# Four weight sums placed elsewhere in the DVE order, and the last sum of h moved between two output sums

## The chip, the cores and the metric

The kernel runs on one core of a Trainium2 chip. The metric is the device time of one execution in microseconds (us). The core has five engines that work through their own instruction streams and wait for each other by semaphores: PE (TensorE, matmuls), DVE (VectorE), ACT (ScalarE), POOL (GpSimd) and SP (SyncE, which issues most transfers).

## What is computed

Retention (attention with a decay instead of a softmax) over 8 batches, 8 heads, 576 positions, 64 features a head. Its output, 4608 tokens of 512 features, goes through four experts, each a two-layer network of width 1024, and the results are summed with weights for each token.

```
scores = (q @ k.T) / sqrt(64)
ret    = scores * where(i >= j, gamma[h] ** (i - j), 0)
x      = (ret @ v), heads side by side            # [4608, 512]
p      = domain_probs / (sum over experts + 1e-9)
for e in range(4):
    h    = maximum(x @ w1[e], 0)                  # [4608, 1024]
    out += p[:, e] * (h @ w2[e])                  # [4608, 512]
```

Inputs and output are float32; the matmuls work on bfloat16.

## The kernel before

**Tiles and stages.** Tokens are cut into 9 blocks of 512 (`nt` 0 to 8). A stage (nt, e) is one block and one expert. Its first layer (x to h, transposed as `hT`) is computed in stage (nt, e); its second layer (h to the output) is computed while PE works on the first layer of the following stage, so that the two alternate on PE.

**Two ways to multiply.** The first stages, up to the first layer of (1,0), are "classical": `up_classical` (L490) and `down_groups` (L538). They consist of 56 groups, numbered 0 to 55, and a list `plan` says which other work is put behind which group. From (1,1) on the first layer is done with a Strassen-like scheme of seven products instead of eight (`up_fast`, L652), the second layer likewise (`Down`, L594), expert by expert as their sums become ready (`begin`, L971). Such products need sums of operands, which DVE makes:
- `weight_sums` (L550) for w1, into `wsum`;
- `down_sums` (L572) for w2, into `dsum`: three sums (L562 to L564), and one difference written back into w2 (L565), each of 128 x 1024 elements;
- `token_sums` (L567) for x, into `tsum`, through the same lines L562 to L565 but with 128 x 512 elements;
- `hidden_sum` (L577) for h: sum 1 (L586), sum 2 (L588), an in-place difference (L590) and sum 4 (L592). Sums 1 and 2 are made in two halves, one for each group of a stage. The second half of sum 1 reads what POOL has just clipped at zero (L686).

**A fast stage.** It has two groups, g = 0 and 1. In each, `up_fast` issues seven up products into the PSUM banks P, Q and R and calls `fill(1)` to `fill(4)` between them, which issue the seven down products of the stage before. The first DVE addition of a group (L677) reads bank P, and PE's third up product into P has to wait until it has. `fill(4)` ends the down products: products 3 and 4, and then `out(0)` and `out(1)` (L647, or L645 for expert 0; its `out(1)` is on ACT, L643), the two output sums that add the result in PSUM to `acc`. The next group's first down product writes the bank that `out(0)` reads. `sums(1)` to `sums(3)` place h sums, steps of the attention, and token sums for the next block (a list `front`) on DVE.

**Buffers that are shared in time.** `dsum` of expert e lies in buffer `w2s_e`. The raw k, q and v of chunk e of batch 1 lie there before (`raw_units(1)`). So the first down sum of expert 1 waits until POOL has cast chunk 1 of batch 1 (L279 for k and q, L281 for v). These casts are issued at group 25 (`begin1`); the loads behind them go through SP's queue.

**Order.** The order on each engine is that of the program: DVE works strictly through its own list. In the classical part `sums_at` puts sum i behind group g. Groups 24 to 31 are the first layer of (0,2), 32 to 35 its second layer (each evacuated by DVE, L524), 36 to 43 the first layer of (0,3), 44 to 47 its second layer, 48 to 55 the first layer of (1,0). The attention of batch 1 runs at groups 39 to 47: transposes `T(c)` at groups 39, 41, 43, 45, and scores, masks (L333), outputs and kv sums one group later. From stage (1,1) on the attention of batches 2 to 7 is a list of steps, `chain`, from which `window` takes the next one that is ready. When none is ready it takes a token sum from `front`.

Of the kernel before, what the change touches and what calls it, by code (L numbers as in the profile page):

```python
# [23 lines left out]
def kernel(  # L24
# [12 lines left out]
    N, E = moe_domain_probs.shape  # L37
# [474 lines left out]
    def downs(nt, e, ring):  # L512

        hT = hTs[nt, e]
        if e == 0:
            acc[nt] = [apool.tile([128, Dm], FP32, tag="acc", name="acc") for _ in range(NSUB)]

        def evacuate(po, ns, cols):
            t = nt * NSUB + ns
            pe, a = probs[:, e, t:t + 1], acc[nt][ns][:, cols]  # L520
            if e == 0:
                nc.scalar.activation(a, po, Copy, scale=pe)
            else:
                nc.vector.scalar_tensor_tensor(a, po, pe, a, op0=MULT, op1=ADD)  # L524
            if e == E - 1:
                eng = nc.scalar if cols.start else nc.sync
                eng.dma_start(out=out[t * 128:(t + 1) * 128, cols], in_=a)

        for ns in range(NSUB):
            w = Dm // 2 if (nt, ns, e) == (n_nt - 1, NSUB - 1, E - 1) else Dm  # L530
            for d in range(0, Dm, w):
                po = bank(ring, [128, w], FP32, "po")
                for fc in range(NFC):
                    nc.tensor.matmul(po, lhsT=hT[:, fc, ns * 128:(ns + 1) * 128],  # L534
                                     rhs=w2_sb[e][:, fc, d:d + w], start=(fc == 0), stop=(fc == NFC - 1))
                    yield None if fc < NFC - 1 else lambda: evacuate(po, ns, slice(d, d + w))
# [30 lines left out]
    def token_sums(nt):  # L567
        x, a, b = xts[nt], slice(0, HT), slice(HT, NT)
        t = tsum[nt] = tpool.tile([128, 3, 2, HT], BF16, tag="ts", name="tsum", bufs=2)
        return right_sums(t, x[:, 0:2, a], x[:, 0:2, b], x[:, 2:4, a], x[:, 2:4, b])  # L570
# [6 lines left out]
    def hidden_sum(nt, e, i, g=None):  # L577

        lo, hi = (slice(2 * g, 2 * g + 2), slice(4 + 2 * g, 6 + 2 * g)) if g is not None else (slice(0, 4), slice(4, 8))
        hT = hTs[nt, e]  # L580
        a11, a12, a21, a22 = (hT[:, k, t] for t in (slice(0, HT), slice(HT, NT)) for k in (lo, hi))
        h = hsum.setdefault((nt, e), {})
        if i != 3 and i not in h:
            h[i] = hpool.tile([128, NFC // 2, HT], BF16, tag=f"hs{i}", name="hsum", bufs=1)
        if i == 1:
            nc.vector.tensor_tensor(h[1][:, lo], a21, a22, op=ADD)  # L586
        elif i == 2:
            nc.vector.tensor_tensor(h[2][:, lo], h[1][:, lo], a11, op=SUB)  # L588
        elif i == 3:
            nc.vector.tensor_tensor(a21, a11, a21, op=SUB)  # L590
        else:
            nc.vector.tensor_tensor(h[4][:, lo], a12, h[2][:, lo], op=SUB)  # L592

    class Down:  # L594
# [40 lines left out]
        def out(self, i, halves=(slice(0, 2),)):  # L635
# [3 lines left out]
            for x in halves:  # L639
# [8 lines left out]
                if self.e == E - 1:  # L648
                    eng = nc.scalar if len(halves) == 1 and x.start else nc.sync
                    eng.dma_start(out=out[t * 128:(t + 1) * 128, cols], in_=a)  # L650

    def up_fast(nt, e, g, fill, window, sums):  # L652

        x, T, w, s = xts[nt], tsum[nt], w1_sb[e], ssum[e]
# [17 lines left out]
        product(R_, lambda k: s[:, 0, k], lambda k: T[:, 0, k], start=True)  # L672
        nc.scalar.activation(m5, R_, Copy)  # L673
        fill(1)
        sums(1)
        product(P, lambda k: s[:, 1, k], lambda k: T[:, 1, k])
        nc.vector.tensor_tensor(R_, P, m5, op=ADD)  # L677
        product(Q, lambda k: w[:, 2 + k, :HF], lambda k: x[:, 2 + k, t0])
        nc.scalar.activation(hT[:, lo, t0], Q, Relu)  # L679
        fill(2)  # L680
        window("ACT")
        sums(2)
        product(P, lambda k: w[:, k, HF:], lambda k: x[:, k, t1])
        h22 = hT[:, hi, t1]
        nc.vector.tensor_tensor(h22, P, m5, op=ADD)  # L685
        nc.gpsimd.tensor_scalar(h22, h22, float("inf"), 0.0, op0=MIN, op1=MAX)  # L686
        product(R_, lambda k: s[:, 2, k], lambda k: x[:, 2 + k, t1])
        nc.scalar.activation(hT[:, lo, t1], R_, Relu)  # L688
        window("ACT")
        fill(3)  # L690
        sums(3)
# [183 lines left out]
    front = []  # L875

    def pool(nt, n):
        for _ in range(n):
            chain.emit("POOL", nt)
# [4 lines left out]
    def at(g, *fs):  # L884
        plan.setdefault(g, []).extend(fs)
# [52 lines left out]
    def sums_at(kind, e, *gs):  # L938
        todo = []
        for i, g in enumerate(gs):  # L940
            at(g, lambda i=i: (todo or todo.extend(kind(e)), todo[i]()))
        return todo
# [1 line left out]
    sums_at(weight_sums, 1, 16, 17, 18, 19)  # L944
    s0 = sums_at(weight_sums, 0, 20, 21, 22)
    sums_at(weight_sums, 2, 26, 28, 30, 31)
    sums_at(down_sums, 1, 32, 33, 34, 35)
    sums_at(weight_sums, 3, 36, 38, 49, 50)
    sums_at(down_sums, 2, 51, 52, 53, 54)
    at(50, lambda: a1().put_krem(nc.gpsimd, a1().qr[:, 1]))  # L950
# [5 lines left out]
    g = 0  # L956
# [14 lines left out]
    begin = {1: (1, 1), 2: (1, 2), 3: (2, 3), 0: (3, 0)}  # L971
# [6 lines left out]
    def pay(nt, e, late=False):  # L978
        for x in owed:
            if x[1] <= (nt, e) if late else x[0] <= (nt, e):  # L980
                owed.remove(x)
                x[2]()
                return True
        return False

    before, gaps = (1, 0), 0
    for nt, e in [(nt, e) for nt in range(1, n_nt) for e in range(E)][1:]:
        fast = before >= begin[before[1]]
        fill_classical = None if fast else downs(*before, "po")
        while pay(nt, e, late=True):  # L990
            pass

        def tokens(t):
            if t < n_nt and t not in tsum and chain.tokens >= (t + 1) * NT:
                front.extend(token_sums(t))

        def between(i):
            nonlocal gaps
            gaps += 1
            tokens(nt + 1)  # L1000
            if i == 3:
                pool(nt, 4 if gaps < 8 else 3 - g)
            if i == 3 or chain.todo["PE"] and "any" in chain.todo["PE"][0][1]:
                chain.emit("PE", nt)
            chain.now += 1

        def fill(i):
            if i == 4:
                chain.put_late()
            if not fast:  # L1010
                for _ in range(4):
                    f = next(fill_classical)
                    if f:
                        f()
            elif i == 1:
                state["d"] = Down(*before, g)
                d().product(1)
                d().product(5)
                d().copy("P1")
                d().copy("m5")  # L1020
            elif i == 2:
                d().product(6)
                d().copy("U")
                d().product(2, slice(0, 3))
            elif i == 3:
                d().product(2, slice(3, 4))
                d().product(7)
                d().add(12)
                d().add(22)
            else:  # L1030
                d().product(3)
                d().product(4)
                d().out(0)
                d().out(1)
            between(i)

        def d():
            return state["d"]

        def sums(i):  # L1040


            old, new = before in hsum, (nt, e) >= begin[e]
            turns = {(0, 1): 0 if old else 2, (0, 2): 0 if old else 1, (0, 3): 1,
                     (1, 1): 2, (1, 2): 1, (1, 3): 1}[g, i]
            if g == 0 and old:
                for a in {1: ((2, 1), (4,)), 2: ((3,),)}.get(i, ()):
                    hidden_sum(*before, *a)
            if g == 1 and new:
                for a in {2: ((1, 0), (2, 0)), 3: ((1, 1),)}.get(i, ()):  # L1050
                    hidden_sum(nt, e, *a)
            for _ in range(turns):
                window("DVE")
            chain.seen.update(chain.done)

        def window(kind):
            if chain.emit(kind, nt) or kind != "DVE":
                return
            if front:
                front.pop(0)()  # L1060
            else:
                pay(nt, e)

        while nt not in tsum:
            tokens(nt)
            if nt not in tsum:
                chain.put_late()
                moved = [chain.emit(k, nt, strict=False) for k in ("POOL", "PE", "DVE", "ACT")]
                assert any(moved), (nt, chain.done, {k: v[:1] for k, v in chain.todo.items()})
        chain.put_late()  # L1070
        while front and e == 0:
            front.pop(0)()
        for g in range(2):
            up_fast(nt, e, g, fill, window, sums)
        before = nt, e
# [49 lines left out]
```

## Time and profile before

| | us |
|---|---|
| median of 3 runs (527.42 to 527.99) | 527.7 |
| the profiled execution | 527.14 |
| its span, first to last instruction | 525.3 |

| engine | busy us | main work |
|---|---|---|
| DVE | 405.0 | additions and sums, masks, evacuations |
| ACT | 297.2 | evacuations with the nonlinearity |
| POOL | 180.8 | casts of k, q, v; clipping of h |

The span is the time between the first and the last instruction in the trace. The time of an execution is a little longer, since it includes what lies around it. Durations are read from this one execution.

Durations of what is touched: the down sums of 128 x 1024 take 0.68 to 1.41 us, the h sum L586 takes 0.41 to 1.25 us (median 0.42), an output sum of 128 x 512 takes about 0.74 us. The mean granted TensorE clock is 0.991 of full speed.

### The profile page before, as it was taken

What the parts mean: (1) busy time and instruction counts of PE and PEld (TensorE: products, weight loads), DVE (VectorE), ACT (ScalarE), POOL (GpSimd) and SP (SyncE); (2) the same over time, 40 slices, a digit from 0 to 9 for tenths busy, and PEclk for the clock granted to TensorE, in tenths of its full rate; (3) what the DMA queues carried; (4) which work ended last, traced back from release to release, by engine and by line L of the source; (5) the groups of instructions that cost most, each with busy time, mean ns of one, the idle gap of its engine ahead of it and who ended that gap; (6) DMA issues with size and microseconds to landing.
All of it is one profiled execution on the core that took longest, in us unless ns stands there. A gap on an engine that the chain in (4) does not pass through costs nothing.

```text
span 525.3 us, 12553 instructions
## 1 busy us (share of the span) xinstructions
PE 505.6 (96%) x4886; PEld 401.4 (76%) x4886; DVE 405.0 (77%) x744; ACT 297.2 (57%) x613; POOL 180.8 (34%) x275
## 2 busy tenths in 40 slices
PE   7999779999999999999999999999999999999995
PEld 3644335578767888888888888888888888888884
DVE  6614267969845889889888987899889987877786
ACT  3452143566546655666666656666666667666661
POOL 6702252634343343334433544353434310000010
PEclk9999979999999999999999999999999999999999
DMA  9999993954273253734384438523972020001002
GB/s 242 191 207 201 209 161 98 184 102 106 47 169 73 52 119 77 179 71 106 64 193 84 85 64 204 92 55 77 196 112 49 11 82 1 1 21 62 2 0 81
DMA packets 149836, 54.23 MB, mean 103 GB/s; under 512 B 131309, under 2 KB 144621, under 8 KB 149777
## 3 DMA queue, kind: packets, MB, share of 16 engines
q1 hardware_dynamic: 142448, 45.05, 40.5%
q0 software_dynamic: 7328, 8.39, 9.4%
q8 instruction: 38, 0.62, 0.5%
q14 instruction: 22, 0.17, 0.1%
HBM read 45.16 MB, written 9.44 MB: 104 GB/s over the span
## 4 chain that ended last, share of the span: by engine, by line
PE 77%; SPq 6%; DMA 5%; DVE 5%; issue 4%; POOL 2%; POOLq 0%; DVEq 0%
PE upP L665 19%; PE downV L616 18%; PE downW L616 12%; PE upR L665 9%; PE po L534 5%; PE upQ L665 5%; SPq L111 4%; PE ph L493 3%; DMA wt<-in_moe_w_dram 2%; DMA raw<-in_k_dram 2%; PE s L328 2%; SPq L105 1%; PE oc L372 1%; PE oc L369 1%; PE kvp L339 1%
## 5 line engine op out<-in xcount | busy, mean ns | idle before, releaser
L686 POOL TENSOR_SCALAR hT<-hT 128x512 bf16<-128x512 bf16 x62 | 38.2, 617 | 267.1 <-DVE hT L685 261.7
L665 PEld LDWEIGHTS <-wt 128*128 128x128 bf16 x992 | 94.9, 98 | 14.4 <-issue 0.5
L616 PEld LDWEIGHTS <-hT 128*128 128x128 bf16 x928 | 90.8, 98 | 12.9 <-issue 2.3
L665 PEld LDWEIGHTS <-wsum 128*128 128x128 bf16 x744 | 72.7, 98 | 11.8 <-issue 2.3
L616 PE MATMUL downV<-wt,hT 128*128 128x256 bf16 x464 | 78.4, 272 | 1.3 <-DVE acc L645 0.9
L665 PE MATMUL upP<-xT,wt 128*128 128x256 bf16 x496 | 74.4, 273 | 0.2
L616 PEld LDWEIGHTS <-hsum 128*128 128x128 bf16 x696 | 68.1, 98 | 8.4 <-issue 0.4
L693 ACT ACTIVATE hT<-upP 128x512 bf16<-128x512 f32 x62 | 37.0, 597 | 52.7 <-PE upP L665 41.1
L677 DVE TENSOR_TENSOR upR<-upP,m 128x512 f32<-128x512 f32 x62 | 43.2, 698 | 30.0 <-PE upP L665 17.3
L688 ACT ACTIVATE hT<-upR 128x512 bf16<-128x512 f32 x62 | 37.0, 597 | 41.4 <-PE upR L665 41.4
L534 PE MATMUL po<-wt,hT 128*128 128x512 bf16 x224 | 53.4, 379 | 0.0
L671 ACT ACTIVATE upQ<-upP 128x512 f32<-128x512 f32 x62 | 36.3, 586 | 26.2 <-PE upP L665 26.1
L685 DVE TENSOR_TENSOR hT<-upP,m 128x512 bf16<-128x512 f32 x62 | 42.7, 689 | 9.2 <-PE upP L665 8.5
L679 ACT ACTIVATE hT<-upQ 128x512 bf16<-128x512 f32 x62 | 37.0, 597 | 21.8 <-PE upQ L665 21.8
L509 ACT ACTIVATE hT<-ph 128x512 bf16<-128x512 f32 x40 | 23.5, 597 | 37.8 <-PE ph L493 37.8
L493 PE MATMUL ph<-xT,wt 128*128 128x512 bf16 (+3 forms) x180 | 38.1, 367 | 6.6 <-DVE acc L524 6.6
L647 DVE SCALAR_TENSOR_TENSOR acc<-downV,probs,acc 128x512 f32<-128x512 f32 (+1 forms) x48 | 34.4, 723 | 9.6 <-PE downV L616 9.4
L665 PE MATMUL upR<-tsum,wsum 128*128 128x256 bf16 x248 | 37.2, 273 | 1.9 <-DVE tsum L562 1.9
L333 DVE TENSOR_TENSOR sT<-s,tri 128x512 bf16<-128x512 f32 x56 | 36.8, 680 | 2.7 <-PE s L328 2.7
L586 DVE TENSOR_TENSOR hsum<-hT 128x512 bf16<-128x512 bf16 x58 | 35.5, 612 | 3.1 <-POOL hT L686 1.5
L673 ACT ACTIVATE m<-upR 128x512 f32<-128x512 f32 x62 | 36.8, 593 | 1.8 <-PE upR L665 1.8
L665 PE MATMUL upP<-tsum,wt 128*128 128x256 bf16 x248 | 37.3, 273 | 0.0
(134 smaller groups left out, 939.3 us busy)
## 6 DMA issues: line engine op xcount, KB each, us to landing
out_dram<-acc SPq DMA_DIRECT2D x32, 256.0 KB, 2.8
wt<-in_moe_w_dram POOLq DMA_DIRECT2D x6, 1024.0 KB, 25.2
raw_k<-in_k_dram SPq DMA_DIRECT2D x24, 256.0 KB, 3.4
raw_q<-in_q_dram SPq DMA_DIRECT2D x24, 256.0 KB, 3.6
raw_v<-in_v_dram SPq DMA_DIRECT2D x24, 256.0 KB, 3.7
raw<-in_k_dram SPq DMA_DIRECT2D x8, 256.0 KB, 5.0
raw<-in_q_dram SPq DMA_DIRECT2D x8, 256.0 KB, 5.5
raw<-in_v_dram SPq DMA_DIRECT2D x8, 256.0 KB, 5.5
```

The costliest lines, as they stand in the source:

```text
L333: nc.vector.tensor_tensor(self.sT[c][:, j], self.s[c][j], tri[:, :].unsqueeze(1).to_broadcast([128, NP, C]), op=MULT)
L493: nc.tensor.matmul(ph[:, ts], lhsT=w1_sb[e][:, dc, fc * 128:(fc + 1) * 128], rhs=xts[nt][:, dc, ts], start=(dc == 0), stop=(dc == NDC - 1))
L534: nc.tensor.matmul(po, lhsT=hT[:, fc, ns * 128:(ns + 1) * 128], rhs=w2_sb[e][:, fc, d:d + w], start=(fc == 0), stop=(fc == NFC - 1))
L616: nc.tensor.matmul(o, lhsT=l[:, k, self.s * 128:(self.s + 1) * 128], rhs=r[:, k], start=(i == 1 and k == 0), stop=(k == NFC // 2 - 1), ski ...
L665: nc.tensor.matmul(ps[:, l], lhsT=wa(kc)[:, f:f + 128], rhs=xa(kc), start=(start and l == 0 and kc == 0), stop=(kc == 1), skip_group_check ...
L673: nc.scalar.activation(m5, R_, Copy)
L677: nc.vector.tensor_tensor(R_, P, m5, op=ADD)
L679: nc.scalar.activation(hT[:, lo, t0], Q, Relu)
L685: nc.vector.tensor_tensor(h22, P, m5, op=ADD)
L686: nc.gpsimd.tensor_scalar(h22, h22, float("inf"), 0.0, op0=MIN, op1=MAX)
L688: nc.scalar.activation(hT[:, lo, t1], R_, Relu)
L693: nc.scalar.activation(hT[:, hi, t0], P, Relu)
```

## The change

Four sums on w2 of expert 1 get other places in the list of groups. The last half of h sum 1 is issued in `fill(4)` between `out(0)` and `out(1)` instead of in `sums(3)`; where the stage before was classical, it comes behind the fill. And in the second group of an expert 3 stage `window` takes a token sum first, if more than one is waiting, before a step of the attention.

```diff
-    sums_at(down_sums, 1, 32, 33, 34, 35)
+    sums_at(down_sums, 1, 42, 43, 44, 48)
...
                 d().product(4)
                 d().out(0)
+                last_sum()
                 d().out(1)
+            if i == 4 and not fast:
+                last_sum()
             between(i)
+
+        def last_sum():
+            if g == 1 and (nt, e) >= begin[e]:
+                hidden_sum(nt, e, 1, 1)
...
             if g == 1 and new:
-                for a in {2: ((1, 0), (2, 0)), 3: ((1, 1),)}.get(i, ()):
-                    hidden_sum(nt, e, *a)
+                for a in (1, 2) if i == 2 else ():
+                    hidden_sum(nt, e, a, 0)
...
         def window(kind):
+            if kind == "DVE" and len(front) > 1 and (e, g) == (E - 1, 1):
+                return front.pop(0)()
             if chain.emit(kind, nt) or kind != "DVE":
                 return
```

## The prediction

> **What bounds the kernel now.** I read the page first (busy shares, the clock row), then the waits, then the chain of waits in the stretch that stands out, then the timelines of the engines there and in the later, repeating stages.
>
> ```profile
> PE 505.6 (96%) x4886; PEld 401.4 (76%) x4886; DVE 405.0 (77%) x744; ACT 297.2 (57%) x613; POOL 180.8 (34%) x275
> PEclk9999979999999999999999999999999999999999
> ```
>
> The PE is the bound: only 19.7 of 525.3 us are without a matmul, so a change pays only where it fills one of those gaps or lifts the clock. One slice of 40 (65.7 to 78.8 us) has a lower clock. The waits name the largest single gap after the start:
>
> ```profile
> DVE dsum L562 <- POOL vm L281: 9.9, 1, 9.9
> PE ph L493 <- DVE acc L524: 6.6, 1, 6.6
> ```
>
> DVE stood 9.9 us before the first down sum, and PE 6.6 us for an evacuation queued behind it. The chain of waits from 54 to 80 us shows the order of causes:
>
> ```profile
> 54.23 9.95 DMA raw<-in_k_dram
> ...
> 66.55 0.62 POOL vm L281
> 67.17 0.02 issue
> 67.19 0.69 DVE dsum L562
> 67.88 0.67 DVE acc L524
> 68.55 0.04 issue
> 68.60 5.46 PE ph L493 x16
> ```
>
> A load of batch 1 lands late, POOL casts its chunk, the third cast frees the buffer that `dsum` of expert 1 takes over, and only then do the sum, the evacuation and the matmuls go. The table of windows gives the PE's loss and the clock:
>
> ```profile
> 62.00:68.60 6.60, 0.01 (x2) 0.00 (x1) 1.41 (x3) 0.00 (x0) 5.10 (x6) 0.76 1.06 213
> 68.60:74.00 5.40, 5.40 (x18) 2.02 (x18) 5.35 (x8) 1.79 (x3) 2.14 (x3) 0.66 1.26 202
> ```
>
> (columns: length, then busy us and count of PE, PEld, DVE, ACT, POOL, then clock, DMA share, GB/s). The stall has no PE work, and the matmuls after it run at 0.66 of the clock.
>
> The repeating stages have small gaps. Near the end of stage (3,1), that is nt 3, expert 1, which also finishes the products of (3,0), the timelines of POOL, DVE and PE have:
>
> ```profile
> 221.93 0.61 POOL L686 TENSOR_SCALAR hT<-hT 128x512 bf16<-128x512 bf16 x1 [4.50 <-DVE hT L685]
> 222.50 1.04 POOL L279 TENSOR_TENSOR km<-raw_k,gk 128x512 bf16<-128x512 f32 x1
> 223.50 1.22 POOL L279 TENSOR_TENSOR qm<-raw_q,gq 128x512 bf16<-128x512 f32 x1
> ...
> 222.57 1.25 DVE L586 TENSOR_TENSOR hsum<-hT 128x512 bf16<-128x512 bf16 x1
> 223.75 0.74 DVE L645 TENSOR_SCALAR acc<-downV,probs 128x512 f32<-128x512 f32 x1
> ...
> 224.54 0.60 PE L616 MATMUL downV<-wt,hT 128*128 128x256 bf16 x4 [0.21 <-DVE acc L645]
> ```
>
> L586 is the sum that moves. It took 1.25 us here, 0.42 in most places; the output sum behind it was late, and PE waited.
>
> **What the skill says, and the trace.** "TensorE: Matmul & The Clock Gate", Part 1, has the array fall to half clock after an idle window of about 3.4 us and return after about 3.4 us of sustained work. The trace agrees: the 6.6 us stall is followed by slow matmuls until about 72 us. "SBUF — State Buffer", Who interferes with whom, says that a DVE instruction with two SBUF inputs and a GpSimd instruction that reads SBUF exclude each other for a whole instruction. L586 has two such inputs; its 1.25 us ends 0.28 after the POOL cast that ran beside it, the time being the rest of the cast and its own 0.42 less overlap: the trace fits. "TensorE: Matmul & The Clock Gate", in its first table, calls VectorE's queue strict FIFO; the evacuation that waited behind L562 shows it.
>
> **Part 1: four down sums move from groups 32-35 to 42, 43, 44 and 48.** No instruction or DMA is added or dropped; in the listed order only DVE changes before 98 us.
> - Removed: the 6.59 us PE wait. Behind it 16 matmuls of 512 columns took 5.46; an earlier run of such matmuls (47.12 us) took 5.34 for 24, so 16 would be 3.56. That is 1.90 from the clock. Together 8.49 us.
> - What is late next: batch 1's transposes (group 39) would come at about 73.9 - 8.5 = 65.4. Casts are fed by loads and don't move: q of chunk 0 ends at 63.0, of chunk 1 at 66.5 (wanted at 68.3), of chunk 2 at 70.3 (wanted at 71.3). Chunk 3 was cast at 76.1 because km waited for kvp, not for its load; freed by an earlier kvp, it follows chunk 2 at about 71 to 75, wanted at 76.6. All have cover, of 1.0 us at the thinnest. Two casts landing later than I put them would give back what exceeds it.
> - The added wait: L562 in its new place comes at about 71, and its buffer is free at 67.2; no wait. Behind it are a transpose copy, masks and evacuations.
> - Where they land: each sum is 0.68 us alone, up to 1.41 beside POOL. DVE between 74 and 91 had gaps of 0.3 to 1.4 us and its consumers lie a group later (copy at 80.4, used at 82.1). I take 0; if cover fails, 0.7 each, 2.1 for three. The fourth enters a full DVE stretch (91.9 to 99.6) ahead of an idle 0.76: 0.68 to 1.26 less 0.76 is at most 0.5; I take 0.1.
>
> **Part 2: the last h sum goes between the two output sums (27 places, and behind the fill in two more).** The first output sum can start 0.64 us after its product's first matmul (499.66 to 500.30 near the end, DVE waiting).
> - Gain: at the end of stages (3,1) to (6,1) the first output sum moves up by 0.69 (223.75 to 223.06). PE's next product started 0.81 after the former instead of 0.44: 0.37 each, 1.5 us for four.
> - Cost: where the first output sum already waited for PE, the h sum filled an idle stretch and now does not. It delays L588, L592 and the next L677 by its pitch, 0.33 alone. L677 must start 0.74 before the third up product; from its idle time and that distance I get the spare: 0.34 in nt 7 and 8 (cost 0), 0.34 into (3,3) and (4,3) and 0.19 into (5,3) and (6,3), where POOL holds the sum longer (pitch 0.55: 0.1 each, 0.4), 0.15 into (3,1), (4,1) and (6,1) and 0.30 into (5,1) (a cast in the way, delay 0.40: 0.25 and 0.1, sum 0.85), 0.09 into the stages (6,0) and (7,0) (0.24 each, 0.5). Into (3,0) PE already waits 0.96 for `tsum`, queued behind: +0.35. Sum 2.1.
> - Net +0.6. Bounds: nothing but the gain, -1.5; or every contended sum at its longest (0.8 more in some 14 places less 0.3 spare, 7.0, less 1.5), +5.5. I take +0.6.
>
> **Part 3: token sums go first in the last group of expert 3.** At most two move up per block, and one attention step moves a slot later on PE in two blocks. No count changes. The stages after them lose one L564 from the crowded start, which pays for the h sum in (4,0) and (5,0), where PE waited 0.09 each. One mask goes before a later L677 that had 0.63 idle and 0.19 spare: covered. 0, bounds -0.5 and +0.7.
>
> **Sum.** -8.49 + 0.1 + 0.6 + 0 = -7.8. The profiled execution took 527.14 (span 525.3), so 519.3; the median of the runs shown, 527.7, is 0.56 above it: 519.9.
>
> **Rivals.**
> - Sums pay: contention moves away with the shift. Part 2 gives its 1.5 and part 3 0.5: 527.7 - 8.5 - 2.0 = 517.2 to 517.7. For it: POOL's casts are over in many places 0.7 us later. Against: spare is 0.15 or less in ten.
> - The casts become the bound: PE arrives 8.5 us earlier at transposes whose data come from the same loads. If a chunk is 3 us later than I put it, with the half clock risked again, 3 to 4 come back: 523.5. For it: load and cast ran back to back until 78 us. Against: the cast times above.
> - Slower: the moved h sum blocks. At the 19 places up to 412 us where POOL still casts, it would have to stand 1.25 each time, of which some 0.25 is spare: 19.0, less 1.5 and 8.5: +9.0, or 536.7. It decides from 0.53 a place beyond the spare ((8.5 + 1.5)/19). For it: it takes 1.25 in ten of them now. Against: in those it starts just behind a cast that POOL has begun, and 0.7 to 1.2 us later that cast is over.
> - The stall stays because something else frees the buffer: no change. The wait names only the cast, which ends before the new place.
>
> **How the numbers follow.** Forecast 0.68 (own range 518.2 to 521.8), sums pay 0.12, casts bind 0.14, slower 0.03, stall stays 0.03. The range reaches down into the first rival, where about half lies under it, and up to where some of the second is left out: 517.6 to 522.6. About 0.2% (1.1 us) can be told from no change here. Faster 0.94, same 0.03, slower 0.03.
>
> **What would show it.** Right: no wait of DVE L562 for POOL, no PE gap near 62 us, clock 1.00 through to the end, the first L665 near 89.5 instead of 97.9; no PE wait on L645; a longer wait before the first upR of stage (3,0). Wrong: PE waits on transposes or SPq between 65 and 90 us, or many short waits of upP for L677.

## The result and the profile after

| | before | after |
|---|---|---|
| median, us | 527.56 (4 runs, 527.41 to 527.99) | 521.48 (4 runs, 521.01 to 521.99) |
| the profiled execution, us | 527.14 | 521.01 |
| its span, us | 525.3 | 519.2 |

The ratio after to before is 0.9884, with a 95% interval from 0.9867 to 0.9901. The forecast was 519.9 with a range of 517.6 to 522.6: the side and the range held, and the median came 1.6 us above the forecast.

The page of the kernel after shows the busy time of the engines and the granted clock in 40 slices:

```profile
PE 503.8 (97%) x4871; PEld 400.7 (77%) x4886; DVE 401.6 (77%) x744; ACT 297.2 (57%) x613; POOL 180.6 (35%) x275
PEclk9999999999999999999999999999999999999998
```

The slice with the low clock near 70 us is gone (for the 8 at the end, the clock falls at 515.9 us, after the last matmul has ended at 513.8). The waits of PE in the kernel before (in total, times, longest, in us) had, beside the 6.6 us for L524:

```profile
PE upR L665 <- DVE tsum L562: 1.9, 2, 1.0
...
PE downV L616 <- DVE acc L645: 0.9, 4, 0.2
```

In the kernel after, the waits for L524 and for L645 are gone, that for `tsum` is longer, and those for L677 and L685 are new:

```profile
PE upR L665 <- DVE tsum L562: 2.3, 2, 1.3
...
PE upP L665 <- DVE upR L677: 0.9, 2, 0.7
PE downV L616 <- DVE acc L647: 0.4, 1, 0.4
PE upP L665 <- DVE hT L685: 0.4, 2, 0.2
```

The windows over the old stall, in the kernel after (length, busy us and count of PE, PEld, DVE, ACT and POOL, clock, DMA share, GB/s):

```profile
62.00:68.60 6.60, 6.55 (x51) 3.30 (x51) 4.19 (x6) 4.21 (x8) 4.74 (x5) 1.00 1.00 203
68.60:74.00 5.40, 5.35 (x61) 2.99 (x62) 4.33 (x8) 3.52 (x7) 4.41 (x5) 1.00 0.98 210
```

PE is busy for nearly all of both stretches (6.55 of 6.60 and 5.35 of 5.40 us), at full clock. To see where each 0.1 us went, I measured the distances between the same PE instructions in each kernel's trace. They start at the first `orem` matmul (the attention's output for the last 64 positions of the first batch, about 60 us), since what lies before it differs by up to 1.5 us between executions whatever the kernel. A group is marked by its first upR matmul. The column of the kernel before has the lengths, the others what each kernel takes more or less, in us:

| stretch on PE | before | after | p1_only | p1_p2 | p1_p3 | choose |
|---|---|---|---|---|---|---|
| `orem` to the transposes of group 39 (the stall) | 14.13 | -8.60 | -8.60 | -8.60 | -8.60 | -8.60 |
| on to the first upR of (1,1) | 24.48 | 0.00 | +0.02 | 0.00 | 0.00 | 0.00 |
| on to the second group of (1,1) | 7.58 | +0.61 | +0.77 | +0.61 | +1.02 | +0.43 |
| on to the second group of (2,3) | 83.47 | -0.19 | +0.01 | -0.18 | +0.02 | +0.02 |
| on to the first upR of (3,0) | 8.37 | +0.33 | 0.00 | +0.33 | 0.00 | 0.00 |
| on to the second group of (8,3) | 309.29 | +1.42 | 0.00 | +1.20 | +1.59 | -1.20 |
| from `orem` to the end of the span | 465.51 | -6.44 | -7.80 | -6.68 | -5.98 | -9.35 |

So the change gained 8.60 at the stall and lost 2.2 elsewhere. The other four columns are experiments. In the stretch to the second group of (1,1), the kernel after, p1_only, p1_p2 and p1_p3 still issue the same instructions: 0.61 to 1.02 there is what one program shows in four executions.

### The profile page after: what moved, and what is told of

Its sections match the earlier page's. It is cut to its first block, busy times and chain, and to the rows that moved or that the text cites. A ratio compares the mean times of both kernels' runs of the same rounds, so it can differ in the third digit from the quotient of the medians.

```text
span 519.2 us, 12541 instructions
## 1 busy us (share of the span) xinstructions
PE 503.8 (97%) x4871; PEld 400.7 (77%) x4886; DVE 401.6 (77%) x744; ACT 297.2 (57%) x613; POOL 180.6 (35%) x275
## 4 chain that ended last, share of the span: by engine, by line
PE 88%; DVE 7%; issue 2%; DMA 1%; ACT 1%; SPq 0%; DVEq 0%
PE upP L665 20%; PE downV L616 18%; PE downW L616 13%; PE upR L665 10%; PE po L534 9%; PE ph L493 7%; PE upQ L665 4%; PE s L328 2%; DVE upR L677 2%; DVE acc L647 2%; PE oc L372 1%; PE oc L369 1%; PE kvp L339 1%; DMA raw<-in_q_dram 1%; DVE hsum L586 1%
## 5 line engine op out<-in xcount | busy, mean ns | idle before, releaser
L677 DVE TENSOR_TENSOR upR<-upP,m 128x512 f32<-128x512 f32 x62 | 43.2, 696 | 25.0 <-PE upP L665 14.4
L534 PE MATMUL po<-wt,hT 128*128 128x512 bf16 x214 | 52.1, 379 | 0.6
L647 DVE SCALAR_TENSOR_TENSOR acc<-downV,probs,acc 128x512 f32<-128x512 f32 (+1 forms) x48 | 34.6, 726 | 21.6 <-PE downV L616 21.5
L685 DVE TENSOR_TENSOR hT<-upP,m 128x512 bf16<-128x512 f32 x62 | 42.7, 689 | 6.7 <-PE upP L665 4.7
L665 PE MATMUL upP<-tsum,wsum 128*128 128x256 bf16 x248 | 37.2, 273 | 0.0
L665 PE MATMUL upQ<-xT,wt 128*128 128x256 bf16 x248 | 37.2, 273 | 0.0
```

Of the source, the lines that this page charges most:

```text
L647: nc.vector.scalar_tensor_tensor(a, src, pe, a, op0=MULT, op1=ADD)
L665: nc.tensor.matmul(ps[:, l], lhsT=wa(kc)[:, f:f + 128], rhs=xa(kc), start=(start and l == 0 and kc == 0), stop=(kc == 1), skip_group_check ...
```

## The experiments

**Which part gives, which takes.** Theory A: Part 1 alone gives the whole gain, and parts 2 and 3 together lose. Theory B: Part 1 gives less, since POOL's casts bind behind the stall, and parts 2 and 3 gain. Two kernels: Part 1 alone, and parts 2 and 3 without it.

```diff
# p1_only: the kernel before, with
-    sums_at(down_sums, 1, 32, 33, 34, 35)
+    sums_at(down_sums, 1, 42, 43, 44, 48)
# p23_only: the kernel after, with
-    sums_at(down_sums, 1, 42, 43, 44, 48)
+    sums_at(down_sums, 1, 32, 33, 34, 35)
```

> Only the four down sums move; the last h sum and the token sums stay as before. Theory A (the gain is all in the head, and the other two parts together lose about 1.7 us after it): 527.6 - 8.6 for the stall and the half clock + 0.9 for the wait of the third up product for L677 in stage (1,1), so 519.9, faster than the whole change by about 1.6. Theory B (the other parts pay, and what is missing of the forecast was lost in the head): 522.5 to 523.5, slower than the whole change.

> The h sum and the token sums as changed, the four down sums at groups 32 to 35 as before. Theory A: the stall of 6.6 us and the half clock are back, and the stages lose 1.7: 529.2. Theory B: 526.0 to 526.6, faster than before.

p1_only: 520.12 us (520.09 to 520.25), ratio 0.985 (0.9833 to 0.9867). p23_only: 528.8 us (528.29 to 529.76), ratio 1.0016 (1.0009 to 1.0022). Theory A. Parts 2 and 3 are a loss by themselves, and Part 1 alone is faster than the whole change. The waits of PE in p1_only:

```profile
PE downV L616 <- DVE acc L645: 0.9, 4, 0.2
PE upP L665 <- DVE upR L677: 0.9, 1, 0.9
```

and in p23_only:

```profile
PE ph L493 <- DVE acc L524: 6.9, 1, 6.9
```

The first has no stall, keeps the four L645 waits, and shows a new wait for L677, which therefore belongs to Part 1. The second has the stall back.

**Parts 2 and 3, one at a time beside Part 1.**

```diff
# p1_p2: the kernel after, without Part 3
-            if kind == "DVE" and len(front) > 1 and (e, g) == (E - 1, 1):
-                return front.pop(0)()
# p1_p3: p1_only, with Part 3
+            if kind == "DVE" and len(front) > 1 and (e, g) == (E - 1, 1):
+                return front.pop(0)()
```

> The whole change without the token sums' precedence. Theory A: nearly all the loss is the h sum's. The waits for L685 near 241 and 296 us go (0.35 each), the waits for L677 in (4,0) and (5,0) become longer, since L564 is back in front of it (0.33 each): within 0.3 of the whole change, 521.5. If the token sums were what loses: 520.2 or less.

> The four down sums and the token sums' precedence, the h sum where it was. Theory A: 519.9 as with the down sums alone, within 0.4, so about 1.4 under the whole change; waits for L645 (0.37 each from start to start, four) are back, and those of L677 after a moved h sum are gone. If the token sums lose by themselves: 520.6 or more.

p1_p2: 521.23 us (520.84 to 522.08), ratio 0.9873 (0.9854 to 0.9891). p1_p3: 521.41 us (520.98 to 521.77), ratio 0.9874 (0.9856 to 0.9891). The first came as expected. The second did not: Part 3, which I had put at nothing, loses 1.59 us from (3,0) on all by itself. The two losses do not add up: 1.20 and 1.59 alone, 1.42 together.

Compared with p1_only stage by stage, Part 2 alone gains 0.30 in each of (3,2) to (6,2), 1.19 in all, and loses 0.21 to 0.24 in each of (3,1) to (6,1) (0.87), 0.33 in each of (4,0) and (5,0) (0.66), 0.17 in (5,3) and (6,3) (0.34) and 0.25 in (6,0) and (7,0) (0.50); nothing else after (3,0) moves by more than 0.04. The timeline of p1_p2 shows the place in (4,0), first DVE, then PE:

```profile
244.82 0.41 DVE L586 TENSOR_TENSOR hsum<-hT 128x512 bf16<-128x512 bf16 x1
245.15 0.74 DVE L647 SCALAR_TENSOR_TENSOR acc<-downW,probs,acc 128x512 f32<-128x512 f32 x1
245.81 0.41 DVE L564 TENSOR_TENSOR tsum<-xT,tsum 128x512 bf16<-128x512 bf16 x1
...
247.00 0.69 DVE L592 TENSOR_TENSOR hsum<-hT,hsum 128x1024 bf16<-128x1024 bf16 x1
247.61 0.69 DVE L677 TENSOR_TENSOR upR<-upP,m 128x512 f32<-128x512 f32 x1
```

```profile
248.35 0.60 PE L665 MATMUL upP<-xT,wt 128*128 128x256 bf16 x4 [0.42 <-DVE upR L677]
```

DVE works with hardly a gap from the output sum to L677. The h sum L586 takes 0.33 between the two output sums (244.82 to 245.15), all that is behind it comes 0.33 later, and PE waits for L677 at the end of that queue.

The gain is not the whole of the wait that goes. In p1_only PE started its next product 0.38 late behind the L645 output sum at each of the four places. In p1_p2 that is gone, but the down product after it, which reads the moved h sum, starts 0.07 late, since that sum now ends later. So 0.30 remains.

What Part 3 does in the same stage is seen in the timeline of p1_p3; first POOL, then DVE, then PE:

```profile
237.37 1.04 POOL L287 TENSOR_TENSOR qrb<-raw_q,gq 64x512 bf16<-64x512 f32 x1
```

```profile
237.59 1.10 DVE L562 TENSOR_TENSOR tsum<-xT 128x512 bf16<-128x512 bf16 x1
...
240.53 0.42 DVE L564 TENSOR_TENSOR tsum<-xT,tsum 128x512 bf16<-128x512 bf16 x1
240.86 0.69 DVE L685 TENSOR_TENSOR hT<-upP,m 128x512 bf16<-128x512 f32 x1
...
242.79 0.68 DVE L333 TENSOR_TENSOR sT<-s,tri 128x512 bf16<-128x512 f32 x1
243.40 0.73 DVE L647 SCALAR_TENSOR_TENSOR acc<-downV,probs,acc 128x512 f32<-128x512 f32 x1
```

```profile
241.60 0.60 PE L665 MATMUL upP<-tsum,wt 128*128 128x256 bf16 x4 [0.19 <-DVE hT L685]
...
244.18 0.60 PE L616 MATMUL downV<-wt,hT 128*128 128x256 bf16 x4 [0.24 <-DVE acc L647]
```

Three things happen. The token sum L562 took the place that a mask had in p1_only; it now stands beside the cast of `qrb` and takes 1.10 instead of 0.50. L685 then starts 1.03 after the up product that it reads, instead of 0.88. (No more instructions stand ahead of L685 than before: the token sums have each moved up one place, into that of the mask.) The attention's matmuls, about 1 us of PE work that in p1_only lay just before the fourth up product into bank P, moved a slot later: PE arrives earlier, L685 later, and that product starts 0.36 late. And the mask that moved now stands ahead of the output sum L647, for which PE waits as well: its next product starts 0.40 late. With Part 2 the output sum comes first and that last wait is gone, which is why the two losses do not add.

**How long the stall must be for the clock to fall.** The first down sum alone goes to group 35 or 34, the others to 42, 43 and 44, so that the stall comes back in part.

```diff
# stall_35 and stall_34: the kernel before, with
-    sums_at(down_sums, 1, 32, 33, 34, 35)
+    sums_at(down_sums, 1, 35, 42, 43, 44)    # stall_34: 34, 42, 43, 44
```

The 3.4 us in both expectations is the idle window of the page on the clock that the prediction names.

> The kernel before, with the down sums at groups 35, 42, 43 and 44: the first still waits for the cast, but fewer evacuations stand behind it, so PE should stop later and for less. The first consumer it holds is the copy of the first transposes: PE stalls about 2.6 us (scores wanted at 67.0, copy done at about 69.6). If an idle time over some 3.4 us is what lowers the clock, it stays at 1.00 and the time is 527.7 - 8.6 + 2.6 = 521.7, with no wait for L677 in (1,1). If the half clock has another cause at that time (loads, the start of the first run of 512-column matmuls), it comes all the same: 523.5 or more.

> The kernel before, with the down sums at groups 34, 42, 43 and 44: one evacuation stands behind the waiting sum. PE should stop at about 63.9 us, when it needs that bank, for 4.6 us. If the clock falls after an idle time over 3.4 us, 1.9 us more are lost: 525.6 and a clock near 0.66 in the 5 us after. If it takes a longer stall: 523.7.

stall_35: 523.99 us (six runs, 523.09 to 526.4; the profiled one is the longest), ratio 0.9937 (0.9917 to 0.9957). stall_34: 526.22 us (525.25 to 527.3), ratio 0.9972 (0.9964 to 0.9981). Both lie above what was expected, stall_35 by 2.3 us: in its profiled execution the stall was 3.70 us, not 2.6, and the clock fell. The PE timelines, first of stall_35, then of stall_34:

```profile
71.54 0.61 PE L328 MATMUL s<-qkT 64*128 64x128 bf16 x8 [3.70 <-DVE qkT L311]
...
74.97 1.92 PE L493 MATMUL ph<-xT,wt 128*128 128x512 bf16 x4
...
77.99 1.04 PE L493 MATMUL ph<-xT,wt 128*128 128x512 bf16 x4
```

```profile
68.95 3.33 PE L493 MATMUL ph<-xT,wt 128*128 128x512 bf16 x8 [4.00 <-DVE acc L524]
...
72.80 1.03 PE L493 MATMUL ph<-xT,wt 128*128 128x512 bf16 x4
```

The same four matmuls take 1.92 at the low clock and 1.04 at the full one. By the clock records of the two traces the full clock comes back at 72.65 in stall_34 and only at 77.7 in stall_35, 3.7 and 6.2 us after work began again. So the stall and its clock belong together, as Part 1's sum had them (6.59 and 1.90), and in this execution a stall of 3.7 us was long enough. It need not be so in each: the profiled execution has the lowest granted clock of its six (0.991, the others 0.995 or 0.996), and the two shortest, of 523.1, leave hardly any room for a slow stretch. That is an estimate: p1_only's 520.1, less the 0.8 that it lost in (1,1), plus the stall of 3.7, makes 523.0.

**The fourth down sum.** In the kernel after it goes on to group 45.

```diff
-    sums_at(down_sums, 1, 42, 43, 44, 48)
+    sums_at(down_sums, 1, 42, 43, 44, 45)
```

> The whole change with the fourth down sum (L565) behind group 45 instead of 48. Theory A (in its place at 48 it stands in a full stretch of DVE and pushes the masks and L677 of stage (1,1)): the wait of the third up product near 94.6 us goes, 0.8 us gained, 520.7. Rival (L677 is late there for another reason, the shift of the casts on POOL against DVE): the wait stays at 0.5 or more and the time within 0.3 of the whole change.

521.2 us (520.37 to 521.98), ratio 0.988 (0.9864 to 0.9897): in medians no difference from the kernel after that can be told. In the trace, the stretch in (1,1) went from 8.19 to 7.75 us, so 0.44 of the 0.61 came back. (The last experiment below has the sum at 45 as well and took 8.01 there; with the sum at 48 four executions took 8.19 to 8.60. The direction holds, the size varies.) The rest is another wait, on the scores' operand, which SP's transposes deliver:

```profile
92.26 0.40 PE L328 MATMUL s<-qkT 64*128 64x128 bf16 x8 [0.21 <-DMA qkT<-km]
```

**Are the losses made by POOL's casts?** In three kernels POOL writes zeros in place of the casts of batches 2 to 7, so that it reads no SBUF there; the attention of these batches is left out in effect (lines from L287 on stand 6 later in these kernels).

```diff
# in cast, and likewise in cast_rem
+            if self.b > 1:
+                eng.memset(o, 0.0)
+                return
```

Theory C: Part 2's loss is one of place in the queue and stays without casts, Part 3's is one of casts and goes. Theory D: Part 3's loss, too, is one of place. For Part 2 the numbers expected under either theory overlap, so there only the places of the losses can decide.

> The down sums alone moved, and for batches 2 to 7 POOL fills the k, q and v tiles with zeros instead of casting them (the attention of these batches is left out in effect; every other instruction stays in its place). POOL then writes in those places and reads no SBUF. It is the base for the other two: from the first upR of (3,0) to that of (8,3), second group, 309.3 us as with the casts, less up to 1.2 if the h sum then no longer delays the output sums behind it (L645 waits gone).

> The same with the h sum between the output sums. Theory C (what the moved sum costs is mostly its wait for a cast that reads SBUF): L586 takes 0.42 everywhere; against its base it loses only where the spare is under 0.33: 0.24 to 0.34 each into (4,0), (5,0), (6,0), (7,0), and about 0.18 into three of (3,1) to (6,1), together 1.2 to 1.7 with no gain left to set against it. Rival D (it is the added instruction in the row, cast or no cast): the same or more.

> The same with the token sums first. With the casts this cost 1.6 us from (3,0) on. Theory C: the first token sum took 1.10 beside a cast; without one it takes 0.42, and the waits for L685 and for the output sum behind it go: within 0.4 of the base. Rival D: the token sums take the place of a mask in a full row and cost 1.2 or more also without a cast.

One execution each: 518.02, 518.24 and 518.99 us. From (3,0) on the last two lose 1.16 and 0.79 against the first (1.20 and 1.59 with the casts). The answers for the tiles (durations in ns: least, median, longest), of nocast_p1, of p1_p3 and of nocast_p1_p3:

```profile
L592 DVE TENSOR_TENSOR hsum<-hT x58: 414/421/427, 101.0 to 502.6; 128x512 bf16<-128x512 bf16 x58
```

```profile
L562 DVE TENSOR_TENSOR tsum<-xT x8: 415/418/1103, 83.2 to 433.1; 128x512 bf16<-128x512 bf16 x8
```

```profile
L568 DVE TENSOR_TENSOR tsum<-xT x8: 412/415/421, 84.5 to 430.6; 128x512 bf16<-128x512 bf16 x8
```

Without casts both sums keep to 0.42 us everywhere, where p1_only had L586 at up to 1.255 and p1_p3 L562 at up to 1.103. The gains and losses change as well. Part 2 has nothing left to gain, because the four L645 waits are gone without it; it loses 0.33 in each of (4,0) and (5,0) and 0.25 in each of (6,0) and (7,0), which makes the 1.16, and 0.34 at (3,0). These are losses of place. The four of 0.21 to 0.24 in (3,1) to (6,1) and the two of 0.17 in (5,3) and (6,3) are gone: they need the casts. So of what Part 2 loses from (3,0) on, 2.37 before its gain, about half (1.21) needs the casts. For Part 3 neither theory holds alone: half its loss goes with the casts, half stays, and that is so of both its waits. In each of two blocks the fourth product into P starts 0.19 late where it was 0.36, and the product behind the output sum 0.24 where it was 0.40. Without casts L685 starts as soon behind the product that it reads as in nocast_p1 (0.87), so the 0.19 that stays there is lost cover: the attention's matmuls are no longer in front. The 0.24 stands behind the moved mask. This division is read from the traces; no run isolates the moved mask.

The fourth down sum's loss needs the casts, too. The DVE timelines of the kernel after and of nocast_p1_p2, both with the sum at group 48:

```profile
87.40 0.88 DVE L562 TENSOR_TENSOR dsum<-wt 128x1024 bf16<-128x1024 bf16 x1
...
89.12 0.98 DVE L564 TENSOR_TENSOR dsum<-wt,dsum 128x1024 bf16<-128x1024 bf16 x1
90.03 1.53 DVE L565 TENSOR_TENSOR wt<-wt 128x1024 bf16<-128x1024 bf16 x1
91.48 1.26 DVE L565 TENSOR_TENSOR xT<-xT 128x512 bf16<-128x512 bf16 x1
92.66 1.28 DVE L333 TENSOR_TENSOR sT<-s,tri 128x512 bf16<-128x512 f32 x2
```

```profile
88.32 0.68 DVE L571 TENSOR_TENSOR wt<-wt 128x1024 bf16<-128x1024 bf16 x1
88.92 0.41 DVE L571 TENSOR_TENSOR xT<-xT 128x512 bf16<-128x512 bf16 x1
91.37 1.29 DVE L339 TENSOR_TENSOR sT<-s,tri 128x512 bf16<-128x512 f32 x2 [2.03 <-PE s L334]
```

Without casts the sums are at 0.68 and 0.41, DVE then stands idle for 2.03 us, and the stretch in (1,1) takes 7.48 us: no loss. In the kernel before, the three sums shown here for `dsum` and `wt` took 0.68, 0.77 and 1.09; pushed 0.60 later by the fourth down sum they meet other casts and take 0.88, 0.98 and 1.53.

**A better version.** If Part 2 gains only behind an expert 0 (where PE waited for L645), the last h sum should go between the output sums there alone.

```diff
# choose: p1_only with the fourth down sum at 45, and
                 d().out(0)
+                if before[1] == 0:
+                    last_sum()
                 d().out(1)
...
+                if i == 3 and not (fast and before[1] == 0):
+                    last_sum()
```

> Down sums at 42, 43, 44 and 45, the last h sum between the output sums only where the stage before is an expert 0 stage (its second output sum is on ACT), in its old place elsewhere, token sums as before. Theory A (those places alone gain 0.29 each, four of them, the others lose): 520.1 of the down sums alone, less 0.9 for L677, less 1.2: 518.0, the fastest. Rival (the gain at those places exists only with the other moves): 519.2.

518.59 us (516.81 to 518.77), ratio 0.9824 (0.9804 to 0.9844), in the same comparison as fourth_45 with 521.2: the fastest of the kernels that do all the work. Its interval overlaps that of p1_only, so it is the trace that tells the two apart. The h sum moves at six places, (3,1) to (8,1). From (3,0) on the kernel gains 1.20, 0.30 in each of (3,2) to (6,2), as Theory A had it, and loses nowhere. The waits of PE:

```profile
PE upR L665 <- DVE tsum L562: 1.9, 2, 1.0
...
PE s L328 <- DMA qkT<-km: 0.5, 1, 0.5
PE downV L616 <- DVE acc L647: 0.4, 1, 0.4
```

The L645 waits are gone and no L677 or L685 wait has come for them; the one new wait is that for the transposes.

## Why the prediction was right in kind and 1.6 us off

The profiled execution after took 521.01 where the sum gave 519.3; from `orem` to the end the kernel gained 6.44 where the sum had 7.8. The other 0.3 lies before `orem`, where executions differ anyway. By its steps:

- Part 1, stall and clock, -8.49: measured -8.60 in every kernel that places the sums so. Right. So was the cover of the casts and transposes: the 24.48 us behind the stall did not change.
- Part 1, fourth down sum, +0.1 with a ceiling of 0.5: measured +0.61, and up to 1.02 in the other executions of the same instructions. Mis-sized. The step took the sum's own duration less an idle 0.76 behind it, and left all other durations as they were. But a sum placed in a full queue shifts those behind it against POOL's casts: 0.60 for itself and 0.20, 0.21 and 0.44 more for the three shown make 1.45, less 0.76 is 0.69.
- Part 2, gain of 0.37 at four places: measured 0.30, so 1.2 instead of 1.5. Mis-sized. The wait for the output sum went in full (0.38 between two starts on PE), but the step left out a consumer of the moved sum itself: the down product on the h sum, which now starts 0.07 late.
- Part 2, costs: +0.35 at (3,0), measured 0.33; 0.85 in the stages (3,1) to (6,1), measured 0.87 in p1_p2 and 1.01 in the kernel after; 0.5 in (6,0) and (7,0), 0.50; nothing in blocks 7 and 8 beyond that. There the reckoning by spare time ahead of L677 held. The 0.4 in expert 3 stages met 0.32 by luck: a delay of 0.55 less its own spares of 0.34 and 0.19, twice each, would be 1.1, and the loss came as 0.16 to 0.17 in (5,3) and (6,3) and nothing in (3,3) and (4,3). A small gain that I had not foreseen came in (1,3) and (2,3), 0.10 each.
- Part 3, "which pays for the h sum in (4,0) and (5,0)" and "covered. 0": this failed. Unpaid, these two stages cost 0.33 each in p1_p2; with Part 3 they cost 0.39 each in the kernel after, and 0.72 each in p1_p3. The step looked at L677 alone as the consumer behind the token sums. It missed that a sum of two SBUF operands took the place of a mask beside a cast, that the attention step moved on PE had been L685's cover, and that the moved mask stands ahead of an output sum.

From the forecast to the trace that is +0.5 for the fourth sum, +0.3 for the gain, +0.8 for the two stages and +0.2 in (3,1) to (6,1), less 0.1 in expert 3 stages, 0.2 for (1,3) and (2,3) and 0.1 at the stall: +1.4, as measured (7.8 less 6.44).

Of the rivals, the stall did not stay, the casts did not bind (nothing was lost behind the stall), the sums did not pay, and where the moved sum blocked PE in p1_p2, it did so by 0.17 to 0.34 a place, never by the 0.53 that would have made the change slower.

## What to carry over

A sum moved ahead on a strictly ordered engine costs every consumer behind it that has no spare: list all of them (here L677, L685, the output sums and the product that reads the moved sum), and count PE work that moves away from in front of a consumer as lost cover. Make such a move only at the places where a wait shows that it pays: four of the 29 places held 1.2 of the 1.4 us of gain. Durations beside another engine's traffic are not constants, so a shift re-deals the overlaps behind it, and an idle gap at the end of a full queue is not spare until the queue has been laid out again.

## What the runs showed of the hardware

What a stall costs in clock depends on when it comes as well as on its length. A stall of 3.70 us in the profiled stall_35 cost more clock (low from 70.9 to 77.7, 6.2 us of it with work) than one of 4.00 in stall_34 (low from 69.2 to 72.65, 3.7 us with work). The low stretches last 6.83 and 3.41 us by the clock records, in the kernel before 6.83. "TensorE: Matmul & The Clock Gate" in the Trainium skill (What's actually happening) has a free-running window of some 3.4 us, and the clock returns after a busy one: the lengths of one and two windows fit. They fit in full if a window does not count as busy when work begins 0.6 us after its start, as in stall_35 (71.54 against 70.9). The 3.41 us before the two falls held about 3.1 us of idle time each, so the clock fell without a window that was wholly idle. No run here shows where the limit lies: of the stalls traced, the shortest after which the clock fell was 3.70 us, and PE's waits of up to 1.3 us in the later stages left it alone.

A POOL instruction that only writes did not slow DVE's sums: in nocast_p1 20 of the 58 sums L586 ran beside a write of zeros, and all 58 stayed between 0.414 and 0.427 us. In p1_only 20 ran into a cast and took 0.58 to 1.255. "SBUF — State Buffer" (Who interferes with whom) says that a DVE instruction with two SBUF inputs contends with a GpSimd instruction that reads SBUF and not with one that only writes it, and the trace agrees. The recorded times do not show the two shut out for a whole instruction, as the prediction put it: all 20 sums ended about 0.28 us after the cast that they ran into, less than the 0.42 that a sum takes alone.
